# Attention rebuilt on 64-row products, with wide loads and evictions

## The chip, the cores and the metric

The kernel runs on one core of one Trainium2 chip. The metric is device time in microseconds of one execution, less being better. The engines are TensorE (PE; its weight loads are listed apart as PEld), VectorE (DVE), ScalarE (ACT), GpSimd (POOL) and SyncE (SP), which here only issues transfers. SPq is SP's queue of transfers.

## The reference

Windowed attention over 4 batches, 8 heads, 576 tokens and 64 dimensions; a first MoE of 8 experts, of which each token takes the best; a second, dense MoE. The first four heads look back 32 tokens, the others at every fourth of the last 128.

```python
rel = pos[:, None] - pos[None, :]
mask_plain = (rel >= 0) & (rel < window)                                    # window = 32, heads 0 to 3
mask_dil = (rel >= 0) & (rel < window * dilation) & (rel % dilation == 0)   # dilation = 4, heads 4 to 7
...
scores = np.where(masks[None, :, :, :], scores, -1000000000.0)
attn = np.exp(scores - np.max(scores, axis=-1, keepdims=True))
attn = attn / (np.sum(attn, axis=-1, keepdims=True) + 1e-09)
x = np.matmul(attn, v)                     # then as tokens x 512 = 2304 x 512
...
logits = x @ w_gate                        # 8 experts; e_idx = argmax, gate_w = its probability
out[mask] = gate_w[mask, None] * eom[mask, e, None] * (np.maximum(x[mask] @ w1[e], 0.0) @ w2[e])
...
h = x @ w_in                               # 512 -> 2048
g = np.maximum(h, 0.0) + np.log1p(np.exp(-np.abs(h)))
return g @ w_out                           # 2048 -> 512
```

## The kernel before

**Attention.** A tile (b, w) is a window of 128 tokens of a batch, with all eight heads; a batch has five (the last has 64 tokens), all in all 20. For a batch, `load_qk` brings q and k of four heads (`half` 0 the plain, 1 the dilated ones) with a token's dimensions along the row, on 96 partitions in rows of 1,536 bytes (for half 1 in two transfers of 48 partitions). `transpose_qk` turns one head: three products of 96 columns for q, three for k, each triple evicted in two halves of 64x288 (L306 on VectorE for q, which also scales; L320 and L326 on ScalarE for k). 128 partitions hold two heads: kT is a block diagonal, two heads with zeros between (`fill_k`), as are the values vP (plain) and vD (dilated, `fill_v`), so that one product of 128 rows serves two heads.

`scores` writes the masks as one product of 512 columns and adds 16 products of 32 stationary and 128 moving columns (L362), each on a strip of 32 columns of the array. `softmax` takes the row maxima (L376), `exps` makes eight exponentials from PSUM, four with sums (L386). `transpose_p` (L393) and `evict_p` (L402) turn the weights, `values` (L421) multiplies by v in 16 products, `normalise` divides (L434 to L444) into a tile x, of which there are three, and puts five stores of it to x_dram on SP's queue (L452, L456). `transpose_x` and `evict_x` (L465, L480, L481) turn x for the gate's logits (L496).

**Order.** The order of every engine but POOL is the program's. The loop has 23 steps; step i holds scores and softmax of tile i, the exponentials and the transposed weights of tile i-1, values and normalise of i-2, and the transposed x of i-3. `some_qk` puts between them the heads of the next batch (QK_AT, and QK_0 during the first batch: eight heads over the five tiles of a batch). `pump` advances the routing of a group of tiles by a few operations at a time, `events` does what is due at a step's place, such as the gather for rank 0. SP takes transfers in the order of the program: a store that waits for its x stands ahead of all loads behind it. Scores have two PSUM tiles, values one.

**Behind it.** The experts are taken in order of their number of tokens; rank 0 is chosen early. Its tokens come gathered from x_dram for the first tiles (`mm_gathered`), and by products with one-hot rows for the latest ones (`mm_late`). Then come the eight ranks of the first MoE (the first product at L850) and the second MoE, whose weights are converted from float64 in the background of the attention too. `warm(k)` issues k products of zeros.

## Time and profile before

| | us |
|---|---|
| times of three runs | 853.57, 859.68, 858.11 |
| median | 858.11 |
| the profiled execution: its span | 853.2 |
| start to the first row maximum | 25.2 |
| tiles 0 to 14, with transposes of the next batch | 99.0 |
| tiles 15 to 19 | 21.8 |
| last row maximum to the first MoE's first product | 40.4 |
| both MoE | 666.8 |

The span runs from the first to the last record of the profiled execution. Its own device time apart from the span is not shown; the span is what the sums are made against. In the rows below, "PE q L314" or "L314" is line 314 of the program, names are the program's without their numbers, out<-in, and x6 is the number of instructions put together. An fp32 product leaves two records, a transpose one. PEclk is the granted clock of TensorE as a share of full speed, DMA share is the mean over the core's 16 DMA engines (it can pass 1 where transfers overlap in the records).

### The profile page before, as it was taken

The numbers are of one execution on the slowest core, as the hardware profiler recorded it, in microseconds if no ns is written. First come the engines' busy times: TensorE is split into PE (matmuls) and PEld (weight loads), VectorE is DVE, ScalarE is ACT, GpSimd is POOL, SyncE is SP. The second block draws the span as 40 slices with busy tenths as digits, with TensorE's granted clock in tenths as the row PEclk, the third lists the DMA queues.
The fourth block names the chain that finished last, engine by engine and source line by source line (L and its number), as shares of the span: only waits on it lengthen the run. The fifth ranks groups of instructions, "written<-read, shape, count | busy, mean of one in ns | idle before, by whom it ended". The sixth has DMA issues, their size and how long they took to land.

```text
span 853.2 us, 15164 instructions
## 1 busy us (share of the span) xinstructions
PE 790.8 (93%) x5564; PEld 717.5 (84%) x5584; DVE 551.9 (65%) x1134; ACT 504.4 (59%) x1135; POOL 197.2 (23%) x183
## 2 busy tenths in 40 slices
PE   7778677699899999999899999999999999999996
PEld 7656556499899999999798888889999999999994
DVE  6766656355246777744579899986666665665653
ACT  4788656434365566556666766665655655655553
POOL 9302032514333435543301212121001001001001
PEclk9999999779999999999999999999999999999999
DMA  9989685605578898765951222131000000001000
GB/s 177 210 163 181 134 134 162 196 23 178 173 237 262 263 303 295 253 209 197 319 164 50 75 75 93 38 111 38 19 1 38 0 1 38 1 1 38 1 0 38
DMA packets 91023, 104.21 MB, mean 122 GB/s; under 512 B 31132, under 2 KB 71452, under 8 KB 90944
## 3 DMA queue, kind: packets, MB, share of 16 engines
q1 hardware_dynamic: 80864, 87.50, 38.5%
q0 software_dynamic: 3888, 10.12, 3.5%
q10 hardware_dynamic: 6192, 5.56, 2.0%
q8 instruction: 46, 0.75, 0.4%
q14 instruction: 33, 0.27, 0.1%
HBM read 83.98 MB, written 19.32 MB: 121 GB/s over the span
## 4 chain that ended last, share of the span: by engine, by line
PE 42%; issue 16%; DVE 8%; ACT 4%; POOL 1%; DMA 1%; SPq 0%; POOLq 0%; DVEq 0%
PE q L1398 4%; PE pg L851 4%; PE pg L852 4%; PE pg L850 4%; PE q L1396 4%; PE q L1397 4%; PE ph L850 3%; PE ph L852 3%; PE ph L851 3%; PE py L850 3%; PE py L851 3%; PE py L852 3%; DVE l L1376 2%; ACT gh L1382 1%; DVE l L1374 1%
## 5 line engine op out<-in xcount | busy, mean ns | idle before, releaser
L712 POOL TENSOR_TENSOR wl<-wr,wh 128x1024 fp32r<-128x1024 f32 (+1 forms) x46 | 98.7, 2153 | 207.3 <-ACT wh L796 108.2
L851 PE MATMUL pg<-xlm,wh 128*128 128x384 f32 x384 | 129.6, 338 | 0.0
L850 PE MATMUL pg<-xhm,wh 128*128 128x384 f32 x384 | 129.4, 337 | 0.0
L852 PE MATMUL pg<-xhm,wl 128*128 128x384 f32 x384 | 129.4, 337 | 0.0
L1398 PE MATMUL q<-wh,gl 128*128 128x512 f32 x288 | 114.0, 396 | 2.2 <-DVE gl L712 2.2
L1396 PE MATMUL q<-wh,gh 128*128 128x512 f32 x288 | 113.9, 396 | 0.5
L1397 PE MATMUL q<-wl,gh 128*128 128x512 f32 x288 | 113.1, 393 | 0.0
L1382 ACT CAST gh<-l 128x384 fp32r<-128x384 f32 x96 | 49.2, 512 | 99.7 <-DVE l L1376 99.7
L850 PE MATMUL ph<-xh,wh 128*128 128x424 f32 (+7 forms) x256 | 81.5, 318 | 5.1 <-PEq L1210 2.6
L767 ACT CAST wh<-wr 128x1024 fp32r<-128x1024 f32 x72 | 75.4, 1050 | 14.8 <-ACT y L873 8.6
L712 DVE TENSOR_TENSOR gl<-l,gh 128x384 fp32r<-128x384 f32 x96 | 57.1, 595 | 41.0 <-ACT gh L1382 38.6
L851 PE MATMUL py<-hl,wh 128*128 128x424 f32 (+7 forms) x256 | 80.2, 313 | 2.4 <-DVE hl L864 2.4
L1405 POOL DMA_INDIRECT out_dram<-o,perm_sb x18 | 18.7, 1036 | 271.9 <-DVE o L263 137.5
L850 PE MATMUL py<-hh,wh 128*128 128x424 f32 (+7 forms) x256 | 81.3, 318 | 0.0
L852 PE MATMUL ph<-xh,wl 128*128 128x424 f32 (+7 forms) x256 | 80.7, 315 | 0.0
L851 PE MATMUL ph<-xl,wh 128*128 128x424 f32 (+7 forms) x256 | 80.5, 314 | 0.0
L852 PE MATMUL py<-hh,wl 128*128 128x424 f32 (+7 forms) x256 | 80.0, 312 | 0.0
L712 DVE TENSOR_TENSOR wl<-wr,wh 128x1024 fp32r<-128x1024 f32 x42 | 62.4, 1490 | 20.4 <-ACT wh L767 20.0
L850 PEld LDWEIGHTS pg<-xhm,wh 128*128 128x128 f32 x384 | 72.1, 188 | 3.9
L851 PEld LDWEIGHTS pg<-xlm,wh 128*128 128x128 f32 x384 | 72.1, 188 | 3.9
L852 PEld LDWEIGHTS pg<-xhm,wl 128*128 128x128 f32 x384 | 72.1, 188 | 0.0
L1367 DVE TENSOR_SCALAR w<-u 128x384 f32<-128x384 f32 x96 | 34.7, 361 | 56.5 <-ACT u L1365 55.7
(203 smaller groups left out, 1728.7 us busy)
## 6 DMA issues: line engine op xcount, KB each, us to landing
wr<-in_moe_w_dram SPq DMA_DIRECT2D x64, 512.0 KB
x2r<-yT_dram SPq DMA_DIRECT2D x12, 384.0 KB
vP<-in_v_dram SPq DMA_DIRECT2D x16, 272.0 KB
praw<-in_moe_w_in_dram SPq DMA_DIRECT2D x8, 512.0 KB
praw<-in_moe_w_out_dram SPq DMA_DIRECT2D x8, 512.0 KB
wr<-in_moe_w_in_dram SPq DMA_DIRECT2D x8, 512.0 KB
wr<-in_moe_w_out_dram SPq DMA_DIRECT2D x8, 512.0 KB
vD<-in_v_dram SPq DMA_DIRECT2D x16, 192.0 KB
```

What stands on the lines that cost most here:

```text
L712: e.tensor_tensor(lo, src, hi.bitcast(F32), ALU.subtract)
L767: (eng or nc.scalar.copy)(d[1], d[0])
L850: nc.tensor.matmul(ps, wh, xh, start=(first and i == 0), stop=False)
L851: nc.tensor.matmul(ps, wh, xl, start=False, stop=False)
L852: nc.tensor.matmul(ps, wl, xh, start=False, stop=(last and i == k - 1))
L1367: nc.vector.tensor_scalar(w_, u, 1.0, None, ALU.add)
L1376: nc.vector.tensor_tensor(l, l, u, ALU.subtract)
L1382: nc.scalar.copy(gT[b, f][0], l)
L1396: nc.tensor.matmul(acc[b, t], gh[:, ts_], wh, start=(f == 0), stop=False)
L1397: nc.tensor.matmul(acc[b, t], gh[:, ts_], wl, start=False, stop=False)
L1398: nc.tensor.matmul(acc[b, t], gl[:, ts_], wh, start=False, stop=(f == NF - 1))
L1405: sc = nc.gpsimd.indirect_dma_start(out=out, out_offset=IndirectOffsetOnAxis(ap=perm_sb[:, b * (BT // P) + t, 0:1], axis=0), in_=o, in_off ...
```

## The change

- **Loads.** A tile of raw q or k holds four heads on 128 partitions (two heads' 64 row blocks below each other, two heads side by side), in rows of 2,304 bytes: one transfer. Eight raw tiles instead of six; the pool of the experts' weights opens at the start.
- **Transposes.** A unit is (half, q or k, group of three columns): three transposes that write 128 partitions and three that write 64, all of 128 columns, and one eviction of 128x384. Twelve units a batch; k's on ScalarE, q's on VectorE but for 9 of 24, which ScalarE takes. kT, vP and vD lose their zeros; POOL makes the few fills left.
- **Products.** Two heads lie on partitions 0 to 63 and 64 to 127, and each product has 64 rows and 32 stationary columns: 32 for scores (64 moving columns) and 48 for values (65 columns for the plain heads, 64 and 1 for the dilated), each on one of eight places of the array. The two heads write to two PSUM banks; the masks are two products of 256 columns; scores have one tile of two banks.
- **Softmax.** VectorE subtracts the scores from the maxima into SBUF, ScalarE makes one exponential of 128x512 in place, in the same step. The sums come from the products.
- **Normalise.** One addition, reciprocal and multiplication a tile; six x tiles. The dilated heads' order of tokens is put right in the logits (an addition more) instead of in `evict_x`, which is one copy.
- **Order.** 22 steps: weights of tile i-1 are turned first, scores of tile i follow, values of i-1 stand in the same step, x of i-2 is turned; events are due a step earlier.

```diff
-    raw_p = rawx.enter_context(tc.tile_pool(name="raw", bufs=6, side="right"))
+    wr_p = rctx.enter_context(tc.tile_pool(name="wr", bufs=RB, side="right"))
+    raw_p = rawx.enter_context(tc.tile_pool(name="raw", bufs=8, side="right"))
-    ps_s = psctx.enter_context(tc.tile_pool(name="ps_s", bufs=2, space=PSUM))
+    ps_s = psctx.enter_context(tc.tile_pool(name="ps_s", bufs=1, space=PSUM))
...
+    VW = D + 2
+    qT = [per_p[i].tile([P, 2, 2, QS], F32, name=f"qT{i}") for i in range(2)]
+    kT = [per_p[i].tile([P, 2, 2, S], F32, name=f"kT{i}") for i in range(2)]
+    vD = [per_p[i].tile([P, 2, 4, 4 * D], F32, name=f"vD{i}") for i in range(2)]
...
+    def fills(i):
+        nc.gpsimd.memset(qT[i][:, 1, :, S:], 0.0)
+        nc.gpsimd.memset(vP[i][:, :, :, D:], 1.0)
         for h2 in range(2):
+            nc.gpsimd.memset(vD[i][64 * h2 + 32 : 64 * h2 + 64, :, 3], 0.0)
...
     def load_qk(b, half):
-            r = raw_p.tile([P, 4, 6 * D], F32, tag="raw", name=f"raw{b}{half}{ti}")[:96]
+            r = raw_p.tile([P, 2, 9 * D], F32, tag="raw", name=f"raw{b}{half}{ti}")
+            src = t[b, 4 * half : 4 * half + 4].rearrange("(y x) (p j) d -> (x p) y (j d)", x=2, j=9)
+            nc.sync.dma_start(r, src)
...
+    def transpose_qk(b, half, ti, g):
+        r = raw[b, half, ti].rearrange("p y e -> p (y e)")
+        ps = ps_t.tile([P, 512], F32, tag="tp", name=f"pqk{b}{half}{ti}{g}")
+        for j in range(3):
+            c = D * (3 * g + j)
+            nc.tensor.transpose(ps[:, P * j : P * j + P], r[:, 8 * D + c : 10 * D + c], identf)
+        for j in range(3):
+            c = D * (3 * g + j)
+            nc.tensor.transpose(ps[:D, P * j : P * j + P], r[:, c : c + D], identf)
+        src = ps[:, : 3 * P].rearrange("q (j x p) -> q x j p", j=3, x=2)
+        dst = (qT, kT)[ti][b % 2][:, half, :, :S].rearrange("q x (p j) -> q x j p", j=9)[:, :, 3 * g : 3 * g + 3]
+        if ti == 1:
+            nc.scalar.copy(dst, src)
+        elif b == 0 or half == 1:
+            nc.vector.tensor_scalar(dst, src, -SCALE, None, ALU.mult)
+        else:
+            nc.scalar.activation(dst, src, AF.Copy, scale=-SCALE)
...
     def scores(b, w):
         i = b % 2
+        s = ps_s.tile([P, 2, 512], F32, tag="s", name=f"s{b}{w}")
+        mask = mask_w[:, 0:1].to_broadcast([P, 4, 64]) if w else mask_0.unsqueeze(2).to_broadcast([P, 2, 2, 64])
+        for h2 in range(2):
+            o = s[:, h2, :256]
+            o = o.rearrange("q (c k) -> q c k", k=64) if w else o.rearrange("q (a c k) -> q a c k", a=2, k=64)
+            nc.tensor.matmul(o, identb, mask, start=True, stop=False, skip_group_check=True)
         for half in range(2):
             nk = 64 if w < 4 or half == 0 else 48
             for hp in range(2):
+                for u in range(4):
+                    for h2 in range(2):
+                        rows = slice(64 * h2, 64 * h2 + 64)
+                        q_, k_ = qT[i][rows, half, hp], kT[i][rows, half, hp]
+                        if half == 0:
+                            n = 4 * w + (u if w < 4 else u % 2)
+                            q0, k0 = 32 * n, 32 * max(n - 1, 0)
+                        else:
+                            q_, k_ = [t.rearrange("q (m r) -> q r m", r=4)[:, u] for t in (q_, k_)]
+                            q0, k0 = 32 * w, 32 * max(w - 1, 0)
+                        c = 64 * (2 * half + hp)
+                        nc.tensor.matmul(
+                            s[32 * u : 32 * u + 32, h2, c : c + nk],
+                            q_[:, q0 : q0 + 32],
+                            k_[:, k0 : k0 + nk],
+                            start=False,
+                            stop=(half == 1 and hp == 1 and u == 3),
+                            skip_group_check=True,
+                        )
         tl[b, w] = dict(s=s)
...
     def softmax(b, w):
         d = tl[b, w]
+        mx = sm_p.tile([P, 2, 4], F32, tag="mx", name=f"mx{b}{w}")
+        p = at_p.tile([P, 4, 2, 64], F32, tag="p", name=f"p{b}{w}")
+        s = d["s"][:, :, :256].rearrange("q h (c k) -> q h c k", k=64)
+        nc.vector.tensor_reduce(mx, s, AX.X, ALU.min)
+        nc.vector.tensor_tensor(
+            p.rearrange("q c h k -> q h c k"), mx.unsqueeze(3).to_broadcast([P, 2, 4, 64]), s, ALU.subtract
+        )
         pump()
+        d["p"] = p
     def exps(b, w):
+        p = tl[b, w]["p"].rearrange("q c h k -> q (c h k)")
+        nc.scalar.activation(p, p, AF.Exp)
...
+        o = ps_o.tile([P, 2, 512], F32, tag="o", name=f"o{b}{w}")
+        d["o"] = o = o[:, :, : 4 * (D + 1)].rearrange("q h (c e) -> q h c e", e=D + 1)
         for half in range(2):
             for hp in range(2):
+                for u in range(4):
+                    for h2 in range(2):
+                        rows = slice(64 * h2, 64 * h2 + 64)
+                        c = 2 * half + hp
+                        lhs = pt[rows, c, 32 * u : 32 * u + 32]
+                        if half == 0:
+                            parts = [(vP[i][rows, hp, max(4 * w + (u if w < 4 else u % 2) - 1, 0), : D + 1], slice(0, D + 1))]
+                        else:
+                            parts = [(vD[i][rows, hp, max(w - 1, 0), D * u : D * u + D], slice(0, D)), (one[rows], slice(D, D + 1))]
+                        for rhs, cs in parts:
+                            nc.tensor.matmul(
+                                o[32 * u : 32 * u + 32, h2, c, cs], lhs, rhs, start=True, stop=True, skip_group_check=True
+                            )
     def normalise(b, w):
         d = tl[b, w]
+        x = at_p.tile([P, 2, 2, 2 * D], F32, tag="x", name=f"x{b}{w}", bufs=6)
         d["x"] = x
+        rc = sm_p.tile([P, 2, 4], F32, tag="rc", name=f"rc{b}{w}")
         x2 = x.rearrange("q a b c -> q (a b c)")
         t0 = b * S + P * w
         nt = P if w < 4 else 64
+        nc.vector.tensor_scalar(rc, d["o"][:, :, :, D], 1e-9, None, ALU.add)
         pump()
+        nc.vector.reciprocal(rc, rc)
         pump()
+        nc.vector.tensor_tensor(
+            x.rearrange("q a h (c d) -> q h a c d", c=2),
+            d["o"].rearrange("q h (a c) e -> q h a c e", a=2)[:, :, :, :, :D],
+            rc.rearrange("q h (a c) -> q h a c", a=2).unsqueeze(4).to_broadcast([P, 2, 2, 2, D]),
+            ALU.mult,
+        )
+        pump()
+        nc.sync.dma_start(x_dram[t0 : t0 + nt, :256], x2[:nt, :256])
+        rows = x_dram[t0 : t0 + nt, 256:].rearrange("(m r) d -> m r d", r=4)
+        for r in range(4):
+            nc.sync.dma_start(rows[:, r], x2[32 * r : 32 * r + nt // 4, 256:])
...
+        nc.scalar.copy(xT[g][:, j], d["xp"])
...
+        lt_ = lt[: 32 * n_].rearrange("q (m r) -> q m r", r=4)
+        nc.vector.tensor_tensor(lt_, lt_, pl[: 32 * n_, 1].rearrange("q (r m) -> q m r", r=4), ALU.add)
...
+    for half in range(2):
+        for g in range(3):
+            for ti in range(2):
+                transpose_qk(0, half, ti, g)
+                warm(WARM[1])
...
-    QK_AT = [2, 2, 2, 1, 1]
-    QK_0 = [0, 1, 2, 2, 3]
+    QK_AT = [3, 3, 2, 2, 2]
+    QK_0 = [1, 2, 3, 3, 3]
...
-    for i in range(n + 3):
+    for i in range(n + 2):
...
-            rctx = ExitStack()
-            K["wr"] = rctx.enter_context(tc.tile_pool(name="wr", bufs=RB, side="right"))
...
+        if 1 <= i < n + 1:
+            transpose_p(*tiles[i - 1])
+            evict_p(*tiles[i - 1])
         if i < n:
             b, w = tiles[i]
             if b + 1 < B:
                 nqk = (QK_AT if b else QK_0)[w]
                 if w == 0:
                     if b == 0:
-                        for j in range(2):
-                            fill_k(1, j, nc.gpsimd)
-                        fill_tail(1)
-                        fill_v(1, nc.gpsimd)
-                    todo += [(b + 1, half, h) for half in range(2) for h in range(4)]
+                        fills(1)
+                    todo += [(b + 1, half, ti, g) for half in range(2) for g in range(3) for ti in range(2)]
                 if w == 2:
                     for half in range(2):
                         load_v(b + 1, half)
                 if w in (1, 3) and b + 2 < B:
                     load_qk(b + 2, w // 2)
-            some_qk(nqk - 1)
             scores(b, w)
-        if 1 <= i < n + 1:
-            exps(*tiles[i - 1])
         events(i, 0)
-        if 3 <= i < n + 3:
-            transpose_x(*tiles[i - 3])
-            evict_x(i - 3)
+        some_qk(nqk - 1)
+        if 2 <= i:
+            transpose_x(*tiles[i - 2])
+            evict_x(i - 2)
             pump()
         events(i, 1)
         if i < n:
             softmax(*tiles[i])
+            exps(*tiles[i])
+        events(i, 2)
+        if 1 <= i < n + 1:
+            values(*tiles[i - 1])
+            normalise(*tiles[i - 1])
+        events(i, 3)
         some_qk(min(nqk, 1))
-        events(i, 2)
-        if 2 <= i < n + 2:
-            values(*tiles[i - 2])
-            normalise(*tiles[i - 2])
-        events(i, 3)
-        if 1 <= i < n + 1:
-            transpose_p(*tiles[i - 1])
-            evict_p(*tiles[i - 1])
+        pump()
         events(i, 4)
         pump()
```

On TensorE, before, in the second tile of batch 1 (s11 its scores, o04 the values and px03 the turned x of batch 0's last tiles, pqk20.. heads of batch 2):

```order
L351 MATMUL s11_937<-mask_a_85,identb_65 128x512
L362 MATMUL s11_937<-kT10_121,qT10_117 32x128 x8
L362 MATMUL s11_937<-kT11_122,qT11_118 32x128 x8
L465 MATMUL px03_964<-identf_64,x03_903 128x128 x4
L314 MATMUL pqk2030_974<-identf_64,raw200_460 128x96 x3
L314 MATMUL pqk2031_980<-identf_64,raw201_462 128x96 x3
L421 MATMUL o040_986<-vP0_123,pt04_919 32x130 x4
L421 MATMUL o041_991<-vD0_125,pt04_919 32x128 x8
L496 MATMUL pl0_1004<-xT0_665,wg_68 32x128 x16
L393 MATMUL pp10_1031<-identf_64,p10_871 128x128 x4
```

and of the change, at the same scores:

```order
L374 MATMUL pp10_1181<-identf_64,p10_1090 128x128 x4
L329 MATMUL s11_1192<-mask_w_86,identb_65 128x256
L344 MATMUL s11_1192<-kT1_121,qT1_119 32x64 x32
L291 MATMUL pqk2011_1227<-identf_64,raw201_483 128x128 x3
L294 MATMUL pqk2011_1227<-identf_64,raw201_483 64x128 x3
L291 MATMUL pqk2002_1235<-identf_64,raw200_481 128x128 x3
L294 MATMUL pqk2002_1235<-identf_64,raw200_481 64x128 x3
L437 MATMUL px04_1243<-identf_64,x04_1143 128x128 x4
L404 MATMUL o10_1255<-vP1_123,pt10_1186 32x65 x16
L404 MATMUL o10_1255<-vD1_125,pt10_1186 32x64
L404 MATMUL o10_1255<-one_78,pt10_1186 32x1
```

The weights of the tile before (pp10) now stand ahead of the scores instead of at the step's end, and its values (o10) follow in the same step, where those of the tile before that stood; the last two rows alternate 16 times.

On SP, before, around the first store of x (raw2.. is q and k of batch 2, vP1 and vD1 the values of batch 1, x00 the first tile's output):

```order
L273 DMA raw201_462<-in_k_dram 96x4x384
L287 DMA vP1_124<-in_v_dram 64x17x64 x4
L291 DMA vD1_126<-in_v_dram 64x3x256
L295 DMA vD1_126<-in_v_dram 48x256
L452 DMA x_dram_60<-x00_597 128x256
L456 DMA x_dram_60<-x00_597 32x256 x4
```

and of the change:

```order
L261 DMA raw201_483<-in_k_dram 128x2x576
L427 DMA x_dram_60<-x00_582 128x256
L430 DMA x_dram_60<-x00_582 32x256 x4
L270 DMA vP1_123<-in_v_dram 64x17x64 x4
L274 DMA vD1_125<-in_v_dram 64x3x256
L278 DMA vD1_125<-in_v_dram 48x256
```

The two rows of vD stand four times in both. The stores of x00 moved ahead of the twelve loads of v1.

## Rows read from the trace of the kernel before

**Rows 1.** The page's busy time by engine: us, share of the span, instructions.

```profile
PE 790.8 (93%) x5564; PEld 717.5 (84%) x5584; DVE 551.9 (65%) x1134; ACT 504.4 (59%) x1135; POOL 197.2 (23%) x183
```

**Rows 2.** Windows: stretch, length, busy PE, PEld, DVE, ACT, POOL (x), PEclk, DMA share, GB/s.

```profile
0.00:25.20 25.20, 20.44 (x166) 18.56 (x168) 15.88 (x30) 11.00 (x18) 23.20 (x51) 1.00 1.08 184
25.20:124.20 99.00, 74.22 (x1237) 59.37 (x1254) 65.63 (x202) 73.69 (x253) 13.09 (x18) 0.95 0.91 164
124.20:146.00 21.80, 17.05 (x309) 12.18 (x309) 13.40 (x57) 15.05 (x68) 7.56 (x8) 1.00 0.60 176
146.00:186.40 40.40, 30.90 (x229) 26.23 (x228) 16.17 (x73) 14.65 (x43) 14.96 (x22) 0.75 0.36 105
160.30:180.70 20.40, 15.99 (x63) 13.69 (x64) 7.24 (x29) 6.07 (x13) 6.34 (x6) 0.50 0.23 71
186.40:853.20 666.80, 648.14 (x3636) 601.12 (x3636) 440.84 (x774) 390.02 (x758) 138.37 (x85) 0.99 0.35 113
```

**Rows 3.** The row maxima, L376: the line's summary, then five in time (start, us).

```profile
L376 DVE TENSOR_REDUCE mx<-s x20: 678/682/692, 25.2 to 146.0; 128x8 f32<-128x512 f32 x20
...
73.09 0.68 DVE L376 TENSOR_REDUCE mx<-s 128x8 f32<-128x512 f32 x1
77.22 0.68 DVE L376 TENSOR_REDUCE mx<-s 128x8 f32<-128x512 f32 x1
...
104.29 0.68 DVE L376 TENSOR_REDUCE mx<-s 128x8 f32<-128x512 f32 x1
108.34 0.68 DVE L376 TENSOR_REDUCE mx<-s 128x8 f32<-128x512 f32 x1
...
124.20 0.68 DVE L376 TENSOR_REDUCE mx<-s 128x8 f32<-128x512 f32 x1
```

**Rows 4.** Waits of VectorE, 0 to 186.4: total us, times, longest.

```profile
DVE x L444 <- DMA x_dram<-x: 13.0, 4, 5.6
DVE x L444 <- remote: 4.5, 1, 4.5
```

**Rows 5.** Timeline of VectorE and of SP's queue: start, us.

```profile
35.89 0.76 DVE L444 TENSOR_TENSOR x<-o,rc 128x256 f32<-128x256 f32 x2
...
54.18 0.37 SPq L452 DMA_DIRECT2D x_dram<-x  x1
```

**Rows 6.** Windows, with values' loads, with q's and k's, with experts' weights.

```profile
15.00:19.00 4.00, 3.53 (x24) 3.18 (x24) 3.85 (x8) 2.31 (x5) 3.75 (x15) 1.00 1.39 170
36.00:40.00 4.00, 2.44 (x46) 1.95 (x46) 3.78 (x8) 3.93 (x12) 0.00 (x0) 1.00 1.11 227
134.00:138.00 4.00, 3.50 (x77) 2.70 (x79) 2.56 (x14) 2.81 (x15) 0.31 (x1) 1.00 1.09 343
```

**Rows 7.** Groups by line and shape, 0 to 186.4: busy us, mean ns, idle before.

```profile
L386 ACT ACTIVATE p<-s,mx 128x64 f32<-128x64 f32 x160 | 40.5, 336 | 1.8 <-DVE mx L376 1.6
L306 DVE TENSOR_SCALAR qT<-pqk 64x288 f32<-64x288 f32 x64 | 39.1, 612 | 9.5 <-PE pqk L314 8.7
L320 ACT COPY kT<-pqk 64x288 f32<-64x288 f32 x32 | 21.5, 673 | 12.2 <-PE pqk L314 11.8
L386 ACT ACTIVATION_READ_ACCUMULATOR p<-s,mx 128x1 f32 x80 | 19.4, 245 | 0.0
L326 ACT COPY kT<-pqk 64x288 f32<-64x288 f32 x32 | 17.8, 555 | 3.8 <-PE pqk L314 3.4
L402 ACT COPY pt<-pp 128x512 f32<-128x512 f32 x20 | 11.8, 589 | 17.1 <-PE pp L393 14.0 <-remote 2.8
```

**Rows 8.** Timeline of TensorE: score products, four and eight records, then a burst.

```profile
90.40 0.32 PE L362 MATMUL s<-kT,qT 128*32 128x128 f32 x4
...
90.40 0.42 PE L362 MATMUL s<-kT,qT 128*32 128x128 f32 x8
...
104.60 1.08 PE L362 MATMUL s<-kT,qT 128*32 128x128 f32 x32
```

**Rows 9.** Timeline of weight loads: transposes of p and of q and k.

```profile
103.80 0.42 PEld L393 LDWEIGHTS pp<-identf,p 128*128 128x128 f32 x4 [0.20 <-issue]
...
107.93 0.53 PEld L314 LDWEIGHTS pqk<-identf,raw 96*128 96x128 f32 x6
```

**Rows 10.** Timeline of TensorE: transposes of q and k at the start, and later.

```profile
6.04 0.71 PE L314 MATMUL pqk<-identf,raw 96*128 96x96 f32 x3 [1.27 <-DMA raw<-in_q_dram]
...
18.70 1.17 PE L314 MATMUL pqk<-identf,raw 96*128 96x96 f32 x6
...
20.38 1.17 PE L314 MATMUL pqk<-identf,raw 96*128 96x96 f32 x6
...
107.95 0.69 PE L314 MATMUL pqk<-identf,raw 96*128 96x96 f32 x6
```

**Rows 11.** Timeline: the last x, and the first product of the first MoE.

```profile
164.64 0.42 DVE L444 TENSOR_TENSOR x<-o,rc 128x256 f32<-128x256 f32 x1 [4.52 <-remote]
...
186.46 0.43 PE L850 MATMUL ph<-xh,wh 128*128 128x424 f32 x1 [0.26 <-issue]
```

**Rows 12.** Timeline of TensorE: three products of 24 columns on the whole array.

```profile
107.85 0.22 PE L577 MATMUL prk<-roh,ones 128*128 128x24 bf16 x3
```

More of the change, by code (lines that the diff above doesn't have):

```diff
@@ L79, in attn_moe_softplus_kernel @@
     first = const.tile([P, NE], F32, name="first")
+    one = const.tile([P, 1], F32, name="one")
     e0nt = const.tile([P, 1], F32, name="e0nt")
@@ L90, in warm @@
             nc.vector.memset(tl["zeros"], 0)
-            tl["warm"] = ps_o.tile([P, 512], F32, tag="o0", name="warm")
+            tl["warm"] = ps_o.tile([P, 2, 512], F32, tag="o", name="warm")
         z = tl["zeros"].bitcast(BF16)
         for _ in range(k):
-            nc.tensor.matmul(tl["warm"][:, :144], z[:, :P], z[:, :144], start=True, stop=True)
+            nc.tensor.matmul(tl["warm"][:, 0, :144], z[:, :P], z[:, :144], start=True, stop=True)
     def consts():
@@ L126, in consts2 @@
         nc.gpsimd.memset(ones, 1.0)
+        nc.gpsimd.memset(one, 1.0)
         nc.gpsimd.memset(lg, 0.0)
@@ L281, in load_v @@
         for h in range(4):
[L282 to L283 removed]
+            h2, hp = h // 2, h % 2
             r = slice(64 * h2, 64 * h2 + 64)
@@ L354, in scores @@
             for hp in range(2):
-                for u in range(4 if w < 4 or half else 2):
-                    if half == 0:
-                        n = 4 * w + u
-                        q0, k0 = 32 * n, 32 * max(n - 1, 0)
-                    else:
-                        q0, k0 = SEG * u + 32 * w, SEG * u + 32 * max(w - 1, 0)
-                    c = 4 * half + 2 * hp
-                    nc.tensor.matmul(
-                        s[32 * u : 32 * u + 32, c : c + 2, :nk],
-                        qT[i][half][:, hp, q0 : q0 + 32],
-                        kT[i][half][:, hp, :, k0 : k0 + nk],
-                        start=False,
-                        stop=(half == 1 and hp == 1 and u == 3),
-                        skip_group_check=True,
-                    )
+                for u in range(4):
[17 more added lines that the diff above has]
+                        )
         tl[b, w] = dict(s=s)
@@ L470, in evict_x @@
     def evict_x(i):
-        b, w = tiles[i]
-        d = tl.pop((b, w))
-        nt = P if w < 4 else 64
-        ps = d["xp"]
+        d = tl.pop(tiles[i])
         g = next(g for g, (t0, t1) in enumerate(GROUPS) if t0 <= i < t1)
@@ L477, in evict_x @@
         if j == 0:
-            xT[g] = xt_p.tile([P, 4, 4, P], F32, tag="xT", name=f"xT{g}")
-        t = xT[g][:, j]
-        (nc.vector.tensor_copy if i < len(tiles) - NW else nc.scalar.copy)(t[:, 0:2, :nt], ps[:, :256].rearrange("q (c t) -> q c t", c=2)[:, :, :nt])
-        nc.scalar.copy(
-            t[:, 2:4, :nt].rearrange("q c (m r) -> q c r m", r=4),
-            ps[:, 256:].rearrange("q (c r m) -> q c r m", c=2, r=4)[:, :, :, : nt // 4],
-        )
-        if nt < P:
-            nc.gpsimd.memset(t[:, :, nt:], 0.0)
+            xT[g] = xt_p.tile([P, 4, 4 * P], F32, tag="xT", name=f"xT{g}")
+        nc.scalar.copy(xT[g][:, j], d["xp"])
     def logits_of(i):
@@ L493, in logits_of @@
         if j == 0:
-            xT["pl", g] = ps_t.tile([P, P], F32, tag="tp", name=f"pl{g}")
+            xT["pl", g] = ps_t.tile([P, 2, P], F32, tag="tp", name=f"pl{g}")
         for c in range(NC):
             nc.tensor.matmul(
-                xT["pl", g][32 * j : 32 * j + 32], wg[:, c], xT[g][:, j, c], start=(c == 0), stop=(c == NC - 1), skip_group_check=True
+                xT["pl", g][32 * j : 32 * j + 32, c // 2],
+                wg[:, c],
+                xT[g][:, j, P * c : P * c + P],
+                start=(c % 2 == 0),
+                stop=(c % 2 == 1),
+                skip_group_check=True,
             )
@@ L903, in acc @@
     def acc(c):
-        if c < 2:
-            xacc[c] = ps_s.tile([P, 512], F32, tag="s", name=f"xacc{c}")
-        else:
-            xacc[c] = ps_o.tile([P, 512], F32, tag=f"o{c - 2}", name=f"xacc{c}")
+        if ("a", c // 2) not in xacc:
+            xacc["a", c // 2] = (ps_s, ps_o)[c // 2].tile([P, 2, 512], F32, tag="so"[c // 2], name=f"xacc{c}")
+        xacc[c] = xacc["a", c // 2][:, c % 2]
     def acc0(c):
```

178 lines of the change are left out of this document (29 added, 149 removed).

## The prediction

> **What bounds the kernel now.** I read the page's busy line first: TensorE works in 93% of the span, the other engines in 65% or less [rows 1]. That average says little about the change, so I cut the span at the places where the attention's steps begin and end, and read busy time, granted clock and DMA share of each stretch [rows 2]. The attention is over at 186.4 us. Behind it TensorE is busy for 648 of 666.8 us, and nothing the change touches runs there: I leave 666.8 us as they are. What can move are the first 186.4 us, in four stretches: start-up (25.2), fifteen tiles beside which the next batch's q and k are turned (99.0), the last tiles without that (21.8), and the tail, in which routing ends and rank 0's tokens are gathered (40.4).
>
> In the 99 us no engine is full: TensorE 74, ACT 74, VectorE 66, and the 16 DMA engines 0.91. The row maxima give the steps: 20 of them, 25.2 to 146.0 [rows 3], 6.6 us each in the first fifteen (99.0 / 15). The step from 104.29 to 108.34 took 4.05, with one head's transposes in it, and that from 73.09 to 77.22 4.13. So the work itself fits into about 4, and some 2.5 us a step are waits. What VectorE waits for shows of what kind: L444, which writes the normalised tile x, waited 13.0 us in four pieces for the stores of an older x [rows 4]. x00 was written at 35.89 and its first store was issued at 54.18 [rows 5], because SP had v's twelve loads ahead of it. And the DMA engines carry q and k at 227 GB/s with share 1.11, the 256-byte rows of v at 170, and weights of 128 full partitions at 343 [rows 6].
>
> **The change, part by part.** I keep two sums: what an engine gains or loses, and what the path that ends a step does.
>
> *ACT and VectorE.* The 160 small exponentials and 80 accumulator reads go (40.5 + 19.4 = 59.9 us), 20 exponentials of 128x512 come; a copy of that size took 0.59 [rows 7], so 12: ACT gains 48. The 128 half evictions (39.1 + 21.5 + 17.8 = 78.4 us) become 48 of 128x384. From 0.56–0.67 for 288 columns I take 0.8: 38 in all, ACT gaining about 13, VectorE 27. VectorE pays for 20 subtractions of 128x512; the reduce that reads the same tile takes 0.68 [rows 3], so 14. Neither engine is then the end of a step; the gain of about 60 and 13 us counts only where it shortens the chain below.
>
> *TensorE, scores and values.* A tile had 16 + 16 products, 32 records each (an fp32 product leaves two). Thirty-two take 26 ns apiece when nothing disturbs them: a burst of 1.08 us less 0.25 of the last one's flight. Eight are 0.42 and four 0.32 [rows 8]: the four, on four strips of 32 columns, start within 0.05 of each other (a record alone is 0.27), then the next four follow 0.10 later. So a record of 128 columns holds its strip for some 104 ns, and strips run side by side. Now there are 32 + 48 products, 64 + 96 records, on half the rows and 64 columns (32 of them on one), at eight places. A record should hold its place 52 ns. (a) Eight at a time: 160 x 6.5 = 1.0, with the second mask product 1.2 us a tile. (b) Four at a time: 2.1. (c) If records can't follow each other faster than the average of now, 26 ns: 4.2. Now it is 64 x 26 = 1.7. Three starts in 0.05 are at most 17 ns apart, which is nearer to (a) and (b) than to (c); I take 1.5.
>
> [...]
>
> *TensorE, transposes.* 64 heads of six transposes of 96 rows become 48 units of six of 128 (two halves, two tensors, three groups, four batches): 0.53 x 128 / 96 = 0.71, and as three of the six write only 64 columns, two changes of shape, at the 0.20 that stood before the transposes at 103.80 [rows 9]: 1.1 a unit. In a step 2.4 units (12 / 5) replace 1.6 heads.
>
> *A step with transposes.* From 4.05: less 0.53, plus 2.4 x 1.1, less 0.2 to 0.5 for the products by (a), plus 0.4 by (b): 5.65 to 6.45; with (c) 8.65. The other limit is the chain, since there is one scores tile now instead of two: products, reduce 0.68, subtraction 0.68, and only then the next scores; exponential 0.6, transposes of p 0.42, copy 0.59, values of the next step. With the products and hand-overs it is about 4.3, and 0.7 to 1 more where units stand between: 5.2. I take 5.9: 15 x 5.9 = 88.5, a gain of **10.5**. Bounds: 78 (changes of shape cost nothing, and the chain's 5.2 sets the step) and 130 (all by (c)). Loads keep up at that pace: q and k in rows of 128 partitions at up to 343 instead of 227 GB/s free about 10 of the stretch's 99 us of transfers (of 7 MB, 31 us become 20).
>
> *The stores.* Six x buffers for three, and stores of x00 ahead of v1's loads on SP: the 13.0 us of VectorE's waits should go. I don't add them: they lie in steps that are held to 5.9 by TensorE afterwards. They are what makes it possible that every step is near the undisturbed one.
>
> *The last tiles.* Four steps without transposes: chain 4.3 each, 17.2 instead of 21.8: **4.6**. Bounds 16 and 23.
>
> *Start-up.* Twelve units in place of eight heads, six warming products with each. Six transposes and six products were 1.68 apart (18.70 to 20.38), the six alone 1.17 where they took 0.69 later [rows 10]: TensorE then ran as at its low clock, whatever the column says (both 1.00). Twelve units at 2.4 are 29 and at 1.2 are 14; now it was 14 (eight at 1.7). The first three transposes start at 6.04, held by a load, and the loads in rows of 128 partitions come sooner. Bounds -4 and +10; I take **0**.
>
> *The tail.* 40.4 us at a clock of 0.75, of which 20.4 at 0.50 [rows 2]. The last x is written at 164.64 after a wait of 4.5, and the first product of the first MoE starts at 186.46 [rows 11]. The pipeline is one step shorter, the events of routing stand a step earlier, the last x has a free buffer, and with less idling the clock may stay up: at 1.0, the 16 us of TensorE's work in the slow 20.4 would be 8. Gain bounded by 0 and 16; I take **12**, of which 4.5 are the wait and some 8 the clock.
>
> *Sum.* 10.5 + 4.6 + 0 + 12 = 27 off the span of 853.2. That is 826 for this execution; its span is 4.9 under the median 858.1 of the runs (853.57 to 859.68; what lies around the span isn't shown), so I subtract from the median: **831**.
>
> **Rivals.** (A) As above: 831, between 812 (steps at 5.2, tail -16, start-up -4) and 846 (steps by (b), tail -5).
>
> (B) Records 26 ns apart, case (c). The fifteen steps are 130 (+31), the last four 5.6 (+0.6 in all), the tail gains 10.5: +21, **879**, slower. Each microsecond that a tile's products add costs 15 to 19; the gain is gone at 1.6 over (a), 2.8 us for 160 records, 18 ns a record. For it: prk's products of 24 to 32 columns stand 25 ns apart [rows 12], on the whole array. Against it: the fours.
>
> (C) The transposes that write 64 columns cost twice. Then three of six are 0.71 instead of 0.36: 2.4 x 0.36 = 0.9 a step, 13 in all, and 2 at the start: **846**. [...]
>
> (D) The tail doesn't shrink, as rank 0's gather or the weights of its expert end it, not TensorE: 27 - 12 = 15 off, **843**. For it: DMA share 0.36 and all engines partly idle there.
>
> (E) The loads are no faster and bound the 99 us still, at 0.91 of 16 engines: 16.6 off, **841**.
>
> **How the numbers follow.** A 0.60, B 0.14, C 0.11, D 0.08, E 0.07. What a measurement can tell is about 1%: 849.5 and 866.7 are the limits. A, D, E and two thirds of C lie under 849.5, with little to spare, so faster 0.76; slower is B and the far ends of the start, 0.14; the same 0.10. Range 815 to 862: it leaves out B, the corner of A where everything is best, and what the start's far bound adds to C or D.
>
> **What would show it.** (1) 32 score products in 0.4 to 0.8 us, eight starts within 0.1: (a) or (b); 1.6 or more: (B). (2) The 64-column transposes as long as the 128s, or shorter: against C. (3) Row maxima of the first fifteen tiles 5.9 apart on average, no wait of x for x_dram. (4) The raw loads above 300 GB/s. (5) The stretch from the last row maximum to the first product of the MoE at 28, clock at 0.9 or more. (6) First row maximum at 21 to 35 us. Wrong would be: a step above 7.3, a tail of 40 or a start past 35.

## The result, and the profile after

The changed kernel takes 860.54 us (median of 20 runs, 857.94 to 867.3), the kernel before 854.32 beside it: a ratio of **1.0066, 95% interval 1.0043 to 1.0089**. I had forecast 831 against 858, a gain of 3%. It is slower by 0.4 to 0.9%: no gain at all, though a difference that one would hardly notice.

The profiled execution has a span of 857.2 us, 4.0 more than that of before. Its stretches, cut at the same events (columns as in [rows 2]):

```profile
0.00:22.70 22.70, 19.18 (x239) 17.82 (x241) 6.12 (x13) 6.41 (x8) 8.02 (x42) 0.92 1.05 223
22.70:131.30 108.60, 91.62 (x2809) 77.77 (x2810) 50.10 (x151) 46.15 (x77) 10.66 (x11) 0.95 0.67 153
131.30:162.50 31.20, 23.44 (x712) 18.81 (x707) 15.35 (x47) 9.47 (x16) 6.90 (x8) 0.84 0.51 151
162.50:192.20 29.70, 23.79 (x317) 19.56 (x315) 16.43 (x64) 11.04 (x22) 11.55 (x19) 0.89 0.28 93
192.20:857.20 665.00, 647.50 (x3636) 601.15 (x3636) 441.75 (x773) 390.39 (x758) 139.53 (x85) 0.99 0.36 113
```

| stretch, us | before | forecast | after |
|---|---|---|---|
| start-up | 25.2 | 25.2 | 22.7 |
| tiles 0 to 14 | 99.0 | 88.5 | **108.6** |
| tiles 15 to 19 | 21.8 | 17.2 | **31.2** |
| tail | 40.4 | 28.4 | 29.7 |
| both MoE | 666.8 | 666.8 | 665.0 |

The start came 2.5 us better than forecast and the tail 1.3 worse. The steps took back all of it: 34 us more than forecast, 19 more than before. VectorE and ScalarE are relieved (50 and 46 us busy in the fifteen tiles, 66 and 74 before), and the waits of [rows 4] are gone: L444 of before, L420 now, waits 0.4 us for the stores. But TensorE is busy 17.4 us longer (13.5 of it in the transposes of q and k, 31.9 against 18.4) and idle for 17.0 of 108.6. The 17.4 is some 2 us too large by my estimate: the trace of before has one record of its mask products beside 20 weight loads (L351). TensorE's idle time from 0 to 190 us (waits by line and cause: total, times, longest):

```profile
PE o L404 <- issue: 11.0, 8, 3.0
PE s L344 <- issue: 5.7, 5, 2.5
PE pp L374 <- ACT p L368: 3.1, 4, 1.4
```

"Issue" means that it waits for nothing that the profile shows. One such place, in the values of a tile (timeline of TensorE), and the DMA queue that carries instructions, in the stretch from 76.9 to 78.7:

```profile
77.14 0.23 PE L404 MATMUL o<-one,pt 64*32 64x1 f32 x5
80.10 0.43 PE L404 MATMUL o<-vD,pt 64*32 64x64 f32 x4 [2.73 <-issue]
```

```profile
q8 instruction: 1, 0.02, 5.5%
```

The products stop in the middle of a row, with no wait that the profile shows. One packet of 16 KB on q8 began at 76.98, landed at 78.56, and the products go on 1.54 us later. The whole kernel reads more code that way, after and before (packets, MB, share):

```profile
q8 instruction: 62, 1.02, 0.6%
```

```profile
q8 instruction: 46, 0.75, 0.4%
```

2809 and 2810 records in the fifteen tiles and 22 packets in the same time are 255 a packet: 16 KB are 256 instructions. An fp32 product is four of them: the 32 score products of a tile leave 64 records and 64 weight loads (L344). Up to the first MoE there are 32 packets now, and 15 before. Two runs below show the same by their packets: 57 for 62 where 64 instructions a tile are left out (1280 in all, five times 256), and 74 where 3072 are added (twelve times 256).

Where TensorE stops tells more. Cut inside its stops, the stretches between them hold whole blocks (columns as in [rows 2]):

```profile
47.00:57.00 10.00, 8.79 (x254) 7.25 (x254) 4.40 (x8) 5.67 (x9) 0.00 (x0) 1.00 0.70 215
106.00:110.00 4.00, 2.94 (x127) 2.53 (x127) 2.29 (x6) 1.12 (x3) 0.00 (x0) 1.00 0.47 124
146.50:152.80 6.30, 3.89 (x128) 3.17 (x128) 2.47 (x5) 1.22 (x2) 2.13 (x3) 0.73 0.31 92
```

With TensorE's semaphore instructions, which these columns leave out (4, 2 and none), that is 512, 256 and 256. So it is for the whole of the steps: 27 blocks of 256 begin there, 13 of them behind a pause of 0.16 to 3.0 us that waits for nothing else (16.0 us together), each at exactly the first instruction of its block. TensorE goes on 1.2 to 1.6 us behind the landing of that block's packet, and none of the 27 blocks was begun less than 1.17 us behind it. So these pauses are waits for code.

The stop also costs afterwards (windows around it, columns as in [rows 2]):

```profile
76.00:78.00 2.00, 1.37 (x91) 1.11 (x90) 1.90 (x3) 0.59 (x1) 0.00 (x0) 1.00 1.38 172
78.00:80.00 2.00, 0.00 (x0) 0.00 (x0) 0.04 (x1) 0.63 (x1) 0.00 (x0) 0.91 1.24 173
80.00:82.00 2.00, 1.90 (x20) 1.77 (x20) 1.27 (x6) 0.08 (x1) 0.00 (x0) 0.50 1.06 213
82.00:84.00 2.00, 2.00 (x50) 1.53 (x53) 0.38 (x4) 1.56 (x3) 0.00 (x0) 0.50 0.79 172
84.00:86.00 2.00, 2.00 (x48) 1.79 (x39) 0.00 (x0) 0.00 (x0) 0.00 (x0) 0.50 0.40 124
86.00:88.00 2.00, 2.00 (x103) 1.81 (x102) 1.89 (x5) 0.59 (x1) 0.00 (x0) 0.89 0.53 87
```

The granted clock goes from 1.00 to 0.50 of full speed behind the idle stretch and is up again at 86 to 88 (0.89), though TensorE is busy all the time between.

### The profile page after: what moved, and what is told of

Same layout as the page of the kernel before. It is cut to its first block, busy times and chain, and to the rows that moved or that the text cites. A ratio compares the mean times of both kernels' runs of the same rounds, so it can differ in the third digit from the quotient of the medians.

```text
span 857.2 us, 18988 instructions
## 1 busy us (share of the span) xinstructions
PE 805.5 (94%) x7698; PEld 735.1 (86%) x7699; DVE 529.8 (62%) x1044; ACT 463.5 (54%) x879; POOL 176.7 (21%) x164
## 4 chain that ended last, share of the span: by engine, by line
PE 47%; DVE 10%; issue 8%; ACT 4%; POOL 1%; DMA 1%; SPq 0%; POOLq 0%; DVEq 0%
PE pg L821 4%; PE pg L822 4%; PE pg L823 4%; PE q L1359 4%; PE q L1357 4%; PE q L1358 4%; PE py L821 3%; PE ph L821 3%; PE py L822 3%; PE ph L823 3%; PE ph L822 3%; PE py L823 3%; DVE l L1337 2%; DVE l L1335 2%; ACT gh L1343 2%
## 5 line engine op out<-in xcount | busy, mean ns | idle before, releaser
L683 DVE TENSOR_TENSOR gl<-l,gh 128x384 fp32r<-128x384 f32 x96 | 57.1, 595 | 41.0 <-ACT gh L1343 40.4
L683 DVE TENSOR_TENSOR wl<-wr,wh 128x1024 fp32r<-128x1024 f32 x42 | 60.3, 1439 | 19.2 <-ACT wh L738 19.2
L1359 PEld LDWEIGHTS q<-wh,gl 128*128 128x128 f32 x288 | 54.1, 188 | 19.7 <-DVE gl L683 8.3
```

What stands on the lines that cost most here:

```text
L683: e.tensor_tensor(lo, src, hi.bitcast(F32), ALU.subtract)
L1359: nc.tensor.matmul(acc[b, t], gl[:, ts_], wh, start=False, stop=(f == NF - 1))
```

## The experiments

Theory F: TensorE waits for its own code. Theory W: only its array time counts. For each profile I counted TensorE's pauses of 0.25 us or more, from the first to the last row maximum, that end 1.2 to 1.6 us behind the landing of a packet of q8 ("code stops"). This count takes in pauses that end with another engine's result (one of 1.87 us in the change, and all of those in two_heads and in the three kernels with the old products). Two columns therefore sort, of the same idle time, the pauses of 0.15 us or more that wait for nothing the profile shows ("issue"): those at the start of a block of 256 instructions, and those beside a train of GpSimd's indirect transfers (from 0.3 us before it to 0.8 us behind). Outside both there are at most 3.0 us of them in any run.

The runs were on several chips, with the kernel before beside each (medians 853.06 to 856.41 there), so kernels are compared by their ratios. The stretches come from one profile of each kernel, and runs of one kernel differ by 4 to 16 us: a difference of a few us between two stretches is no more than a hint.

| kernel | steps, us | code stops, us | other idle, us | at a block, us | beside GpSimd, us | tail, us | ratio to before (95%) |
|---|---|---|---|---|---|---|---|
| before | 120.8 | 0.5 (1) | 29.0 | 0.4 (1) | 4.6 | 40.4 | |
| after | 139.8 | 17.5 (12) | 7.2 | 16.0 (13) | 0 | 29.7 | 1.0066 (1.0043 to 1.0089) |
| two_heads | 132.6 | 1.3 (1) | 18.1 | 0 | 1.0 | 28.7 | 0.9969 (0.9941 to 0.9998) |
| two_heads_early | 125.2 | 0 | 12.8 | 0 | 3.3 | 37.0 | 1.0026 (0.9992 to 1.006) |
| sums_on_dve | 136.2 | 7.8 (6) | 19.0 | 9.4 (8) | 5.5 | 35.5 | 1.0058 (1.0027 to 1.0089) |
| sums_shifted | 137.8 | 6.9 (6) | 21.9 | 5.5 (4) | 7.7 | 37.8 | 1.0141 (1.0081 to 1.0201) |
| after_plus | 159.3 | 8.5 (7) | 19.1 | 9.1 (8) | 8.3 | 34.9 | 1.0386 (1.0339 to 1.0433) |
| after_early | 147.3 | 15.4 (11) | 12.6 | 11.3 (9) | 7.2 | 39.7 | 1.0316 (1.0251 to 1.038) |
| no_narrow | 151.7 | 12.7 (9) | 23.5 | 12.4 (9) | 8.9 | 32.4 | 1.0164 (1.0111 to 1.0216) |
| before_x5 | 124.1 | 2.4 (2) | 23.2 | 0 | 5.1 | 32.3 | 0.9964 (0.9929 to 0.9999) |
| before_x5_raw | 118.5 | 0.8 (1) | 20.3 | 0 | 3.9 | 35.4 | **0.9921 (0.9886 to 0.9956)** |

**Products for two heads again** (two_heads).

```diff
                 for u in range(4):
-                    for h2 in range(2):
...
-                            s[32 * u : 32 * u + 32, h2, c : c + nk],
+                        s[32 * u : 32 * u + 32, c : c + 2, :nk],
                         q_[:, q0 : q0 + 32],
-                            k_[:, k0 : k0 + nk],
+                        k_[:, :, k0 : k0 + nk],
```

> The changed kernel with one part undone: scores and values again as products of 128 rows for two heads (block diagonals with their zeros, 16 + 16 products a tile, scores of one bank in two buffers), k's eviction in two halves of 64 partitions, the dilated sums by one VectorE reduce; five x tiles, seven raw tiles, two p and two pt, and the weights' pool opened late, for want of room. Wide loads, wide transposes, one exponential and the shorter pipeline stay. Theory F (TensorE waits for its own code, of which 64-row products are four instructions each): the idle time of the first fifteen steps falls from 17 to about 6 us and of the last four from 8 to 3, and products cost 8 less: about 22 to 25 less than the change, 836 to 839. Theory W (the change costs array time alone): 8 to 10 less, 850 to 852, the idle time unchanged.

852.65. The code stops went from 17.5 to 1.3, as F said, but not the time: TensorE was busy 93.7 us in the fifteen tiles, not 84, and another wait stood behind the stops:

```profile
PE pp L382 <- ACT p L376: 12.2, 12, 2.6
```

The 32 score records take 1.15 us from first start to last where they took 0.81 before, and all of it is in the dilated heads (0.69 for 0.35; the plain ones 0.46 in both), whose queries and keys now lie four apart. So F's mechanism is borne out, its price in time is not: of the 16 us of stops that went, 11 came back as other idle time. By the ratios the run is 8 us below the change, which is W's figure (8 to 10), though not for W's reason: of the 7.2 us that the steps lost, TensorE's work is 1.8 and its idle time 5.4.

**Softmax ahead of the transposes**, in both forms.

```diff
+        if i < n:
+            softmax(*tiles[i])
+            exps(*tiles[i])
         some_qk(nqk - 1)
```

> The kernel of the run with products for two heads, with softmax and exponential of a tile put ahead of the transposes of q, k and x in the step, so that VectorE's reduce no longer stands behind an eviction of q. In that run TensorE waited 9.6 us in eleven pieces for the exponential (transposes of p). Theory D (the order on VectorE makes that wait): it goes, 6 to 9 less, 843 to 847. Rival W (TensorE's work of 93.7 us in 107 sets the pace): no more than 2 less, 851 or above.

854.34. The wait for the exponential fell from 12.2 to 2.3 us, and the steps from 132.6 to 125.2: D is right in its place. But the tail grew from 28.7 to 37.0, its clock fell from 0.88 to 0.77, and the sum stayed; D's 6 to 9 us didn't come. Half of the tail's growth is work at that clock (27.7 us busy for 23.2), half idle time (windows of the tail, this run and the one before it):

```profile
148.20:185.20 37.00, 27.68 (x192) 23.08 (x191) 19.27 (x68) 11.04 (x22) 14.91 (x22) 0.77 0.41 85
```

```profile
157.90:186.50 28.60, 23.19 (x190) 18.93 (x188) 17.09 (x68) 11.10 (x22) 13.37 (x20) 0.88 0.31 88
```

> The changed kernel with the same reordering. There TensorE waits only 3.1 us for the exponentials; D: 0 to 3 less, 858 to 860. F: the stops in the products of scores and values, 1.4 to 1.6 us behind the landing of 16 KB of code, stay where they were in number and length.

880.86, a miss by 20: steps 7.5 longer, tail 10.0. The code stops stayed, as F had it (11 for 12, 15.4 us for 17.5). In the steps there are 7.2 us of pauses beside GpSimd's transfers, of which the change has none. Why the tail grew so is open; no run separates it.

**Less and more work for TensorE.**

```diff
-                            parts = [(vD[i][rows, hp, max(w - 1, 0), D * u : D * u + D], slice(0, D)), (one[rows], slice(D, D + 1))]
+                            parts = [(vD[i][rows, hp, max(w - 1, 0), D * u : D * u + D], slice(0, D))]
...
+        nc.vector.tensor_reduce(rc[:, :, 2:].rearrange("q h c -> q c h"), d["p"][:, 2:], AX.X, ALU.add)
```

> The changed kernel without the 16 products of one column a tile; VectorE sums the dilated weights in one reduce. 64 instructions (4 KB) of TensorE less a tile. W: the 9 us of array time that they own (6.6 in the first fifteen tiles, 2.3 in the last four), so 851. F: besides, five fetches of 16 KB fewer at 0.75 us: 847. If neither is on the path: 860.

860.34, the same as the change; both theories missed, and the figure for neither came by another way. The code stops fell (17.5 to 7.8, by place 16.0 to 9.4), yet 11.8 us of other idle time came. About half of it, 5.5 us, stands beside GpSimd's transfers; what that looks like, the timelines of TensorE and GpSimd in the next run show:

> The run with the dilated sums on VectorE, with the routing of a group begun six turns of the pump later; work and code are the same. Theory P (while GpSimd sends a group's places by indirect transfers, products of TensorE come in handfuls 0.6 to 0.7 us apart, so that it matters which products that phase meets): the time changes by 3 us or more either way, as other bursts of scores and values are met, and the long bursts move with the phases. If the meeting doesn't matter: within 2 of that run, relative to the kernel before.

```profile
122.79 1.12 PE L344 MATMUL s<-kT,qT 64*32 64x64 f32 x43
124.33 0.44 PE L344 MATMUL s<-kT,qT 64*32 64x64 f32 x4 [0.42 <-issue]
125.05 0.44 PE L344 MATMUL s<-kT,qT 64*32 64x64 f32 x3 [0.28 <-issue]
125.78 0.46 PE L344 MATMUL s<-kT,qT 64*32 64x64 f32 x5 [0.29 <-issue]
127.23 0.46 PE L344 MATMUL s<-kT,qT 64*32 64x64 f32 x5 [0.99 <-issue]
```

```profile
123.04 0.91 POOL L585 DMA_INDIRECT idx_dram<-pair,rposi  x1 [34.18 <-DVE rgs L563]
124.25 0.96 POOL L585 DMA_INDIRECT idx_dram<-pair,rposi  x1 [0.30 <-issue]
125.52 0.95 POOL L585 DMA_INDIRECT idx_dram<-pair,rposi  x1 [0.30 <-issue]
```

864.44 against 860.34 with the same instructions: ratios 1.0141 and 1.0058, whose intervals touch. A row of score products that takes 0.81 us elsewhere takes 6.0 while GpSimd sends the places of a group's tokens. The other rows that come in such handfuls lie in these phases too, in this profile from 84, 123 and 153 on, and from 169 beside the gathers for rank 0. Which rows they meet, a shift of the routing decides. This supports P, and the table does so better than the time: GpSimd's trains cover 17 to 22 us of the steps in every run, and hold most of the "issue" pauses that stand at no block. But a meeting alone does not make them: in the change seven rows of products stand beside such trains and took 0.7 to 1.9 us, without such a pause. What else it takes is open. In time the two profiles differ by 1.6 us in the steps, and that the later routing itself lengthened the tail by 2.3 us is not excluded.

```diff
+        for _ in range(10):
+            nc.tensor.matmul(tl["oo"][:, 0, 320:464], z[:, :P], z[:, :144], start=True, stop=True, skip_group_check=True)
```

> The changed kernel with ten products of zeros (128x144, about 0.06 us each) behind the values of each tile, into columns that nobody reads: 0.6 us of array time a tile, 12 in all, with twenty instructions. W (TensorE's work sets the pace of a step): 10 to 12 more, 870 to 873. Theory C (what TensorE does less comes back as idle time at a lower clock, what it does more is paid back by a clock that stays up): 0 to 5 more, 860 to 866, and less time at the low clock.

885.35: 27 us more than the change by the ratios, for 12 us of work by my estimate (0.06 us a product; at the start of before such products stand 0.12 us apart, L94), so W is missed by 15. In the profile TensorE is busy 16.7 us longer in the steps and 5.6 in the tail, more than the products were reckoned at, and 8.3 us of pauses beside GpSimd's transfers came. So TensorE's work does count, and theory C is wrong in this direction: time at the low clock did not shrink, it grew (0.94 in the fifteen tiles for 0.95, 0.75 in the tail for 0.89). The code stops halved, which fits F, as the rows of products stand further apart.

```diff
-            nc.tensor.transpose(ps[:D, P * j : P * j + P], r[:, c : c + D], identf)
```

> The changed kernel without the 144 transposes that write 64 partitions (the scores of two of four heads are then of the wrong tokens). Their array time is 13.7 us in the first fifteen steps and about 6 us in the start. W and F: 14 to 17 less, 844 to 846, as TensorE sets the pace of those steps. If the chain through VectorE and ScalarE sets it: less than 6, above 854.

870.29, some 25 above what both theories had, and the steps longer by 12, with less work: the clock in the fifteen tiles was 0.85 (0.95 in the change), and 8.9 us of pauses stand beside GpSimd's transfers. This run says less than the others: without those transposes the scores differ, and so other tokens go to other experts. It shows that less work of TensorE need not shorten the steps.

**A probe of the code's supply** (code_rate).

> A probe: the changed kernel with 1536 weight loads of 128x32 that nobody uses, in a row, ahead of the fourth tile, and as many again behind the last product of the second MoE: 96 KB of code each, nothing to wait for. F (16 KB of code, 256 instructions, come no faster than one every 2 to 3 us): in the rows the loads run in groups of 256 at their own pace, with stops of 1 us or more between, so 12 to 18 us for each row of 1536; longer in the middle, where other transfers run, than in the end. W (code always arrives in time): one even spacing, no stop above 0.3 us.

957.05 in a single run, span 955.5. Both rows took 44 to 46 us instead of F's 12 to 18, and that in the middle ran evenly, as W had it. But F isn't tested at the pace of the products: a lone weight load took 29 ns (18 in the first hundred), so 256 of them 7.4 us, longer than a packet and the 1.4 us behind it need. The row at the end showed something else. Weight loads that wait for nothing, beside GpSimd's transfers of the output:

```profile
906.43 1.84 PEld L1426 LDWEIGHTS <-identb 128*32 128x32 bf16 x96
908.43 0.33 PEld L1426 LDWEIGHTS <-identb 128*32 128x32 bf16 x9 [0.17 <-issue]
909.18 0.30 PEld L1426 LDWEIGHTS <-identb 128*32 128x32 bf16 x8 [0.41 <-issue]
909.90 42.76 PEld L1426 LDWEIGHTS <-identb 128*32 128x32 bf16 x1423 [0.43 <-issue]
```

```profile
908.20 0.96 POOL L1369 DMA_INDIRECT out_dram<-o,perm_sb  x1 [0.30 <-issue]
```

The first 96 ran on undisturbed, though a transfer was issued beside them too (906.93 to 907.89), as did 43 records of products and as many loads in sums_shifted. Behind them came eight or nine instructions each 0.72 to 0.75 us until shortly after the next transfer had been issued, then one every 30 ns. These loads wait for no data, so I take it that the supply of instructions stumbles. A code packet was under way there as well (908.50 to 910.27); in sums_shifted none was from 124.66 on, and the handfuls went on to 128.7.

**The stores and loads alone, in the kernel before.** The first line of the diff is in both runs (with v's loads behind the stores), the other in before_x5_raw.

```diff
-        x = at_p.tile([P, 4, 2, D], F32, tag="x", name=f"x{b}{w}")
+        x = at_p.tile([P, 4, 2, D], F32, tag="x", name=f"x{b}{w}", bufs=5)
...
-                if w in (1, 3) and b + 2 < B:
+                if w in (0, 2) and b + 2 < B:
```

> The kernel before with five x tiles instead of three (two p and pt instead of three) and the loads of v issued behind the stores of x in the step. Theory S (the waits for stores were on the path): VectorE's 13.0 us of waits go, 8 to 13 less: 841 to 846. Rival (the loads of q and k set the pace there): no more than 3 less, and the waits of L306 and L320 for transposes grow.

851.75: 0.4% faster, 3 us by the ratio (4.7 by the medians), about the rival's bound and far from S. The waits for stores went, and those for raw tiles came in their place (16.8 us, 7.3 before):

```profile
PE pqk L314 <- DMA raw<-in_k_dram: 10.7, 5, 3.0
PE pqk L314 <- DMA raw<-in_q_dram: 6.1, 2, 4.1
```

> The kernel before with five x tiles and v's loads behind the stores, as in the run of that name, and q and k of the batch after next loaded at the first and third tile of a batch instead of the second and fourth. There TensorE waited 12.1 us in five pieces for raw q and k. Theory L (the loads of q and k, that is their place on SP's queue, set the pace once x has room): 4 to 8 less than that run, 843 to 848. Rival (the DMA engines, 0.89 busy there, are full and the loads only displace others): within 2 of that run, and the waits for raw tiles stay above 8.

846.18, 0.8% faster than before and 1.4% than the change, both clear of noise. The same waits in this run:

```profile
PE pqk L314 <- DMA raw<-in_q_dram: 4.5, 2, 2.4
PE pqk L314 <- DMA raw<-in_k_dram: 4.2, 3, 2.2
```

The waits halved, as L had it. Its step in time isn't shown apart: by the ratios this run is 3.7 us below before_x5, where L wanted 4 to 8, and the two intervals overlap. What is shown is the sum: with room for x and the loads earlier in SP's queue, the old products and transposes are the better ones.

## Why the prediction was wrong

**What failed: "What VectorE waits for shows of what kind", and from it "every step is near the undisturbed one".** I took the 2.5 us of waits in a step for waits of data, and had them vanish with the stores and loads. They did: L444's 13.0 us became 0.4. But I had no term for TensorE's own code. I counted records (64 to 160 a tile) for their array time only. At four instructions a product the 80 products need 20 KB a tile, and the waits for code are 16.0 us of the 34 that the forecast missed. The rest is 9 us of other idle time and 9 more of TensorE's work, 6 of them in the last tiles. What the waits for code cost in time is less sure: without them (two_heads) the kernel was 8 us faster, as other waits took their place. The 2.5 us were also too much from the start: TensorE was busy 74.2 us in before's fifteen steps, 4.9 each and not 4.05, so that a step of 6.6 held 1.7 of idle time at most. How late code is read the trace shows: in the steps of the change a packet began when 0 to 229 instructions (median 137) were left to issue ahead of the block it carries. Values issue 192 in 1.04 us, and a packet took 0.9 to 3.2 us.

**Right: TensorE's work in a step.** I took 5.9; 91.6 us in fifteen steps are 6.1. That it came so close is in part luck, as its parts were off in both directions. (One sum of mine was wrong: 4.05 - 0.53 + 2.64 + 0.4 is 6.56, not 6.45, and (A)'s far end 848, not 846.) Score products, now (timeline; compare [rows 8]):

```profile
114.57 1.10 PE L344 MATMUL s<-kT,qT 64*32 64x64 f32 x64
```

64 records in 1.10 less 0.25 are 13 ns apiece: case (b), and exactly the time of before's 32. Case (c), which had 26, did not come. But 13 is a mean of two. The same row's first half, the plain heads, after and before:

```profile
114.57 0.46 PE L344 MATMUL s<-kT,qT 64*32 64x64 f32 x32
```

```profile
104.60 0.64 PE L362 MATMUL s<-kT,qT 128*32 128x128 f32 x16
```

By their starts the plain half takes 0.27 us now and took 0.46, some 8 ns a record, near case (a); the dilated half takes 0.54 and took 0.35. Its queries and keys lie four elements apart since the transposes leave the tokens in order. In two_heads, with before's products on this layout, it takes 0.69. So halving the rows did gain array time in both halves; the new layout of the dilated heads took it back, and the code doubled. A unit of transposes:

```profile
68.94 0.55 PE L291 MATMUL pqk<-identf,raw 128*128 128x128 f32 x3
69.33 0.49 PE L294 MATMUL pqk<-identf,raw 128*64 128x128 f32 x3
69.65 0.60 PE L437 MATMUL px<-identf,x 128*128 128x128 f32 x4
```

From 68.94 to 69.65 are 0.71, what the columns ask for by my estimate (0.53 x 128 / 96); the two changes of shape that I had added at 0.2 each are not there, and the narrow three cost no more than the wide (0.32 us from 69.33 on, the wide 0.39 from 68.94), against rival C: that they cost twice was a supposition, which no run shows. So the transposes are cheaper than I took them, and masks and the values' products of one column dearer. The loads bounded nothing, against E: TensorE waited 2.2 us for raw tiles, and from 88 to 92 us, with raw rows and stores of x under way, 342 GB/s were moved.

**Wrong: the last tiles.** 17.2 forecast, 31.2 measured. I left out the logits, which are due a step earlier and fell into this stretch, and the clock (0.84); 23.4 us busy and 7.8 idle, of that 5.6 code stops. The logits are busy 5.1 us there, 2.0 before.

**Right: start-up and tail.** The start is at 22.7 (bounds 21 to 35). The tail is at 29.7 with a clock of 0.89 for 0.75, near the 28.4, and TensorE is busy 23.8 us in it for 30.9, near the 8 that I had put to the clock. That this comes from the change is only argued: kernels with the same tail lie between 28.7 and 39.7, and not by the clock alone (37.8 at 0.90 in sums_shifted, 35.5 at 0.76 in sums_on_dve).

**The chances.** Slower had 0.14, for B's reason; what came was B's sign by another mechanism, at a quarter of its size. Same had 0.10, and by the 1% that I named, this is where the result lies.

## What to carry to other kernels

Count instructions and their bytes beside array time when a product is split: here the rows of small products ran at 11 to 13 ns a record (values: 96 in 1.04 us, scores: 64 in 0.85), their code came in packets of 16 KB on a queue of its own, and the stops for it (16.0 us in the steps) show as "issue" in the middle of a row, whole blocks of 256 instructions apart. Keep a layout out of the same step, or count it by itself: here its loss (dilated heads, 0.35 to 0.54 us a tile) hid the gain of the split (plain heads, 0.46 to 0.27). Before rebuilding a stage whose waits are for buffers and loads, try the buffer and the queue's order alone: five x tiles and an earlier load gave 0.8% here, the rebuilding none. And judge a tuned stage with what follows it: time won in the steps came back in a longer tail at a lower clock in two of these runs (two_heads_early: 37.0 us at 0.77 for 28.7 at 0.88 in two_heads; sums_on_dve: 35.5 at 0.76 for 29.7 at 0.89 in the change; one profile each).

## What the runs showed of the hardware

- TensorE waited for its own code: in the steps of the change 13 of 27 blocks of 256 instructions (16 KB) began behind a pause of 0.16 to 3.0 us (16.0 together), at exactly the block's first instruction and 1.2 to 1.6 us behind the landing of its packet on the instruction queue. With about half the records (3470 for 7038 in the steps), no block did (two_heads).
- In trains of GpSimd's indirect transfers (0.96 us each), TensorE's instructions came eight or nine at a time each 0.7 to 1.5 us, even weight loads that wait for nothing; the first 96 of these ran on undisturbed. A row of score products took 6.0 us there instead of 0.81. That the one causes the other is inferred: most "issue" pauses away from a block's start stand beside these trains (1.0 to 8.9 us of the steps in ten profiles), but rows beside them in the change took only 0.7 to 1.9 us.
- After a stop of 2.7 us the granted clock was 0.50 of full speed from 80 to 86 us, for 1.00 up to 78, at full work (the change).
- Products of 32 columns on different places of the array started 8 ns apart on average (64 rows, plain heads: 32 records in 0.27 us), and 17 ns apart where their operands lie four elements apart (dilated heads: 0.54 us; the change).
